# Batch 0 of a pooled-attention kernel: k by head pair over SyncE's queue, half of q over ScalarE's, v in two halves

## The chip, the cores and the metric

The kernel runs on one core of a Trainium2 chip. A core has five engines that run their own instruction streams and wait for one another by semaphores: PE (TensorE, matrix products into PSUM), DVE (VectorE) and ACT (ScalarE) for elementwise work, POOL (GpSimd), and SP (SyncE), which here only issues transfers. SP, ACT and POOL can issue DMAs; here POOL's DMAs also convert float32 to bfloat16 on the way, those of SP and ACT copy as is. The metric is the time of one execution in microseconds (us). The profiler also gives the span, from the first to the last instruction, and every start time below is counted from its beginning. All sizes in KB are those written on the chip.

## The reference

Attention over 8 batches and 8 heads of 576 tokens with head size 64, in which keys and values are first averaged over groups of 8 tokens (72 groups), and then a two-layer network on the 4608 tokens:

```python
k_p = k.reshape(B, H, Sp, pool, D).mean(axis=3)      # B=8, H=8, Sp=72, pool=8, D=64
v_p = v.reshape(B, H, Sp, pool, D).mean(axis=3)
scores = (1.0 / np.sqrt(D)) * np.matmul(q, k_p.transpose(0, 1, 3, 2))
scores = scores - np.max(scores, axis=-1, keepdims=True)
attn = np.exp(scores)
attn = attn / (np.sum(attn, axis=-1, keepdims=True) + 1e-09)
attn_out = np.matmul(attn, v_p)                      # (8, 8, 576, 64)
x = attn_out.transpose(0, 2, 1, 3).reshape(4608, 512)
h = x @ w_in                                         # 512 -> 2048
g = h * np.cos(h)
out = g @ w_out                                      # 2048 -> 512, float32
```

Inputs and output are float32.

## The kernel before

The order of the instructions on each engine is written out by hand: no scheduler moves them, and each engine takes its own in the order of the program.

**The network.** The 4608 tokens are cut into 9 tiles of 512 (`NT`), the loop variable being `t`. For a tile, `up_mm` multiplies `w_in` in 8 pieces (`fp`), each of two 128-row chunks with 4 products over k (`ki`), into one of three double banks of PSUM (`banks`); `up_g` takes the cosine on ACT and multiplies on DVE into `g_sb`. Then `down_mm` runs 64 products with `w_out` into two single banks (`obanks`), and `down_out` copies and stores. The attention of the next batch is set between these products. The weights come in four quarters each: `w_in_sb0..3` and `w_out_sb0..3`. For tile 0 the down products are ordered so that a quarter of `w_out` is first asked for at the products 0, 8, 16 and 24.

**The attention.** Batch b's result `xT` is needed by tile b (and a piece of tile b+1). Scores are worked out in four units (`us`, here by heads: two stretches of 256 tokens for heads 0 to 3, then the two for heads 4 to 7) and a rest of 64 tokens that is done later. A unit is: `scores` (products on PE, then the exponential on ACT, `ex`); `sums_first` (the denominators by PE with a matrix of ones, then logarithm and exponential of its negative on ACT, `lnc` and `inv`; there is a single `lnc` buffer); `values_then` (products with pooled v on PE, then a multiplication by `inv` on DVE into `xT`). For the later batches pooling runs on POOL; for batches 0 and 1 it runs on PE:

- `pool_k_mm` multiplies the staged k of a head pair with `groups`, a matrix of zeros and ones that DVE builds at the start (`dist`, `sign`, `groups`) from two iotas of POOL. Both halves of the partitions (a head each) land in one bank, and `put_kk` copies them into `kk`, each half into both halves of the partitions: four copies for a call of two head pairs.
- `pool_v_mm` does the same for v, 18 products of 256 columns, and one copy into `vz`.
- `q_transpose_mm` transposes 128x128 blocks of q on PE into PSUM; a copy puts them into `qT`.

**The beginning.** Before tile 0 nothing can be hidden behind the network. In the order of the program (L336 to L423): SP loads the first half of k (head pairs 0 and 1) as float32 into `k_first`, a part of `g_sb` that is not yet used, and ACT casts it in one operation (L343). POOL issues, on one queue, which works them off in order: the first half of q, then after its iotas the second halves of k and q, v whole, the first three quarters of `w_in`, k of batch 1, and so on, `w_out` last (L344 to L386). An issue on POOL waits until the eighth DMA before it has landed. PE warms up with products that nobody reads (`warm_up`, first ten, later pairs), pools the first two head pairs of k, transposes the first half of q (copies on DVE and ACT), does the scores of units 0 and 1, the second half of k and of q, and the rest as it lands (L396 to L422).

Of the kernel before, what the change touches and what calls it, by code (L numbers as in the profile page):

```python
# [9 lines left out]
FP32 = mybir.dt.float32  # L10
BF16 = mybir.dt.bfloat16
# [3 lines left out]
POOL = 8  # L15
# [4 lines left out]
def kernel(  # L20
# [9 lines left out]
    nc = tc.nc  # L30
# [94 lines left out]
    def v_part(b):  # L125
        return vz[b % 2][:, :, 0:4:3, :]

    def put_kk(b, ps, pj0, pj1, copy):
        dst = kk[b % 2].rearrange("p (j a) n -> p j a n", a=2)
        for a in range(2):  # L130
            for r in range(2):
                copy(out=dst[half[r], pj0:pj1, a, 0:Sp], in_=ps[half[a]])

# [16 lines left out]
    def pool_k_mm(b, bank, pj0, pj1):  # L150

        kb = staged["k", b]
        ps = bank[:, 0:(pj1 - pj0) * Sp].rearrange("p (j n) -> p j n", n=Sp)
        for pj in range(pj0, pj1):
            for t in range(ROW):
                for rows in half:
                    nc.tensor.matmul(ps[rows, pj - pj0, :], lhsT=kb[rows, pj, t, :], rhs=groups[rows, t, :],
                                     start=(t == 0), stop=(t == ROW - 1))
        return lambda copy: put_kk(b, ps, pj0, pj1, copy)

    def pool_v_mm(b, pair):
# [122 lines left out]
    def exp_tables():  # L284
        nc.scalar.preload_act_table_set("natural_log_exp_and_others")  # L285
# [49 lines left out]
    warm = consts.tile([128, 512], BF16, name="warm")  # L335
    nc.vector.memset(warm, 1.0)  # L336
    exp_tables()
# [3 lines left out]
    k_first = g_sb.rearrange("p f n -> p (f n)").bitcast(FP32)[:, 0:2 * ROW * D]  # L341
    nc.sync.dma_start(out=k_first.rearrange("p (j n) -> p j n", j=2), in_=even_view(k, 0, 0, 2))
    nc.scalar.copy(out=staged["k", 0][:, 0:2].rearrange("p j t d -> p (j t d)"), in_=k_first)  # L343
# [11 lines left out]
    load_even(staged["v", 0], 0, v)  # L355
# [5 lines left out]
    nc.vector.tensor_tensor(out=dist, in0=row_of.unsqueeze(2).to_broadcast([128, ROW, Sp]),  # L361
                            in1=first_of.unsqueeze(1).to_broadcast([128, ROW, Sp]), op=mybir.AluOpType.subtract)
    nc.vector.scalar_tensor_tensor(out=sign, in0=dist, scalar=1.0 - POOL, in1=dist, op0=ADD,
                                   op1=mybir.AluOpType.mult)
    nc.vector.tensor_scalar(out=groups, in0=sign, scalar1=0.0, scalar2=None, op0=mybir.AluOpType.is_le)
# [5 lines left out]
    nc.vector.memset(half_pi, math.pi / 2.0)  # L371

# [9 lines left out]
    load_even(staged["v", 1], 1, v)  # L382
    for i in range(2):
        nc.gpsimd.memset(kp2[i], 0.0)  # L384
# [3 lines left out]
    def warm_up(n, bank):  # L388

        for i in range(n):  # L390
            nc.tensor.matmul(bank, lhsT=warm[:, 0:128], rhs=warm)
# [27 lines left out]
    values_then(0, us[2], obanks[1])  # L419
    values_then(0, us[3], obanks[0])  # L420
# [4 lines left out]
    for t in range(NT):  # L425
# [41 lines left out]
        if t == 0:  # L467
            fill[1:] = [(2, S_(0, 0)), (8, lambda: pool_v_mm(1, banks[1])), (8, lambda: values(t, REST, banks[2])),
# [66 lines left out]
```

The softmax here doesn't subtract the row's maximum and nothing guards it: scores larger than these inputs give would overflow.

## Time and profile before

| what | us |
|---|---|
| median of five runs | 302.57 |
| the five runs | 302.82, 307.39, 302.57, 302.21, 302.37 |
| the profiled execution | 302.82 |
| its span | 301.0 |
| PE busy in the span | 292.9 |
| ACT busy / DVE busy | 206.0 / 171.7 |

In the beginning of the profiled execution:

| event | us |
|---|---|
| SP issues the first half of k; it lands 3.6 later | 0.75 |
| POOL issues the first half of q; it lands 6.2 later | 1.27 |
| PE's first warm-up product | 1.47 |
| PE pools the first half of k | 5.58 |
| PE transposes the first half of q | 7.55 |
| ACT's first exponential (unit 0) | 9.31 |
| ACT's last `inv` (unit 3) begins | 17.64 |
| PE begins the up projection of tile 0 | 17.19 |
| PE begins the down projection of tile 0 | 33.56 |
| PE has the second quarter of `w_out` | 38.21 |

A line of the timeline gives start, length, engine, line of the kernel, operation, output and inputs, form and count, and in brackets how long the engine had stood idle and who released it. A line of the waits gives the engine and what it worked on, what it waited for, the total, the number of times and the longest. A line of the stages gives the stretch, its length, the busy time of PE, PE's weight loads, DVE, ACT and POOL with counts, the granted share of PE's clock, the busy share of the DMA engines and the GB/s written. PE's busy time is modelled and overlaps, so it is no measure of how well PE is used.

### The profile page before, as it was taken

Reading aid. Unit: us, or ns where it says so; the run is one execution under the profiler, and the core shown is the slowest. Engines: PE = TensorE matmul, PEld = TensorE weight load, DVE = VectorE, ACT = ScalarE, POOL = GpSimd, SP = SyncE. Lnnn points to the kernel's source line nnn. Section 1 sums busy time; section 2 is a strip of 40 time slices with the busy share of each in tenths; the row PEclk is TensorE's granted clock in tenths of the full one; section 3 lists DMA queues with packets and bytes.
Section 4 is the critical chain, followed back from the end, with each engine's and each line's share of the span. In section 5 each row is a group of like instructions: output and inputs, shape, how many; then the busy total and the mean of one; then the engine's idle time right before and its main releaser. Section 6 shows DMA issues by size and latency. Waiting matters only on the chain.

```text
span 301.0 us, 4620 instructions
## 1 busy us (share of the span) xinstructions
PE 292.9 (97%) x1814; PEld 142.7 (47%) x1814; DVE 171.7 (57%) x212; ACT 206.0 (68%) x255; POOL 129.8 (43%) x92
## 2 busy tenths in 40 slices
PE   7799999999999999999999999999999999999995
PEld 2545544444544554445444544455444544444444
DVE  6558537575467446754675556654775477425712
ACT  3886897469866987688768886789668966605500
POOL 8543016993983398339913990389300000000000
PEclk9999999999999999999999999999999999999999
DMA  7999999629526951796079617791911130131023
GB/s 144 204 207 206 209 203 200 144 46 176 121 68 119 168 123 35 142 163 138 5 167 149 127 32 171 95 174 38 149 24 35 37 70 0 37 70 35 0 67 75
DMA packets 44165, 32.91 MB, mean 109 GB/s; under 512 B 22128, under 2 KB 39408, under 8 KB 44144
## 3 DMA queue, kind: packets, MB, share of 16 engines
q0 software_dynamic: 19744, 18.07, 38.4%
q1 hardware_dynamic: 24160, 14.42, 20.5%
q8 instruction: 14, 0.23, 0.3%
q10 hardware_dynamic: 240, 0.13, 0.2%
q14 instruction: 7, 0.06, 0.1%
HBM read 36.70 MB, written 9.44 MB: 153 GB/s over the span
## 4 chain that ended last, share of the span: by engine, by line
PE 86%; DMA 10%; POOL 2%; issue 0%; DVE 0%; POOLq 0%
PE obank L310 40%; PE bank L297 37%; DMA w_out_sb<-in_moe_w_out_dram 6%; PE bank L241 5%; DMA w_in_sb<-in_moe_w_in_dram 4%; PE bank L211 3%; PE bank L328 1%; POOL kv_st L84 1%; POOL kp L384 1%; POOL q_b L84 1%; POOL identity masks.py:197 0%; POOL row_of L348 0%; DVE o_sb L316 0%; POOL identity masks.py:199 0%; POOL first_of L351 0%
## 5 line engine op out<-in xcount | busy, mean ns | idle before, releaser
L310 PE MATMUL obank<-w_out_sb,g_sb 128*128 128x512 bf16 x560 | 131.4, 379 | 0.5 <-DMA w_out_sb<-in_moe_w_out_dram 0.5
L297 PE MATMUL bank<-xT,w_in_sb 128*128 128x512 bf16 x576 | 126.7, 379 | 0.0
L304 ACT ACTIVATE cos<-bank,half_pi 128x1024 f32<-128x1024 f32 x72 | 79.2, 1112 | 59.0 <-PE bank L297 59.0
L307 DVE TENSOR_TENSOR g_sb<-bank,cos 128x1024 bf16<-128x1024 f32 x72 | 87.3, 1223 | 42.5 <-ACT cos L304 42.5
L297 PEld LDWEIGHTS <-w_in_sb 128*128 128x128 bf16 x576 | 56.1, 98 | 67.7 <-issue 1.8
L310 PEld LDWEIGHTS <-g_sb 128*128 128x128 bf16 x560 | 52.9, 98 | 57.1 <-issue 2.5
L252 DVE TENSOR_TENSOR xT<-bank,inv 64x512 bf16<-64x512 f32 (+1 forms) x72 | 45.3, 630 | 41.3 <-ACT inv L248 40.6
L141 POOL TENSOR_TENSOR kv_st<-kv_st 72x2048 f32<-72x2048 bf16 x12 | 48.8, 4064 | 35.2 <-DMA kv_st<-in_k_dram 35.2
L247 ACT ACTIVATE lnc<-bank 64x512 f32<-64x512 f32 (+1 forms) x72 | 39.2, 544 | 3.2 <-PE bank L241 1.9
L316 DVE COPY o_sb<-obank 128x512 f32<-128x512 f32 x35 | 23.6, 690 | 31.0 <-PE obank L310 30.6
L218 ACT ACTIVATE ex<-bank 72x1024 bf16<-72x1024 f32 (+1 forms) x40 | 35.0, 928 | 8.9 <-PE bank L211 8.9
L142 POOL TENSOR_TENSOR kv_st<-kv_st 72x1024 f32<-72x1024 f32 x12 | 28.2, 2346 | 1.0
L248 ACT ACTIVATE inv<-lnc 128x512 f32<-128x512 f32 (+1 forms) x36 | 21.0, 583 | 1.1
L241 PE MATMUL bank<-ex,vz 72*128 72x256 bf16 (+1 forms) x176 | 20.0, 243 | 0.0
L241 PEld LDWEIGHTS <-vz 72*128 72x128 bf16 x176 | 13.6, 97 | 9.6 <-DVE xT L252 0.5
L145 POOL TENSOR_TENSOR kp<-kv_st 72x512 bf16<-72x512 f32 x12 | 15.0, 1266 | 0.5
L211 PE MATMUL bank<-qT,kk 64*72 64x256 bf16 (+1 forms) x192 | 13.4, 252 | 0.7 <-ACT qT L193 0.5
L211 PEld LDWEIGHTS <-kk 64*72 64x72 bf16 x192 | 7.5, 109 | 10.6 <-issue 7.9
L285 ACT ACT_TABLE_LOAD x9 | 11.5, 1283 | 0.9 <-PEq L519 0.8
L499 POOL COPY gate<-kk 1x1 bf16<-1x1 bf16 x5 | 0.9, 180 | 25.1 <-DMA kk<-kp 25.1
L288 ACT ACT_TABLE_LOAD x9 | 11.5, 1283 | 0.2
L84 POOL DMA_DIRECT2D q_b<-in_q_dram x10 | 7.7, 772 | 2.8 <-DMA w_in_sb<-in_moe_w_in_dram 1.4
(55 smaller groups left out, 89.2 us busy)
## 6 DMA issues: line engine op xcount, KB each, us to landing
out_dram<-o_sb SPq DMA_DIRECT2D x70, 128.0 KB, 2.4
kv_st<-in_v_dram POOLq DMA_DIRECT2D x8, 576.0 KB, 13.8
kv_st<-in_k_dram POOLq DMA_DIRECT2D x7, 576.0 KB, 7.6
q_b<-in_q_dram POOLq DMA_DIRECT2D x6, 576.0 KB, 9.8
w_in_sb<-in_moe_w_in_dram POOLq DMA_DIRECT2D x4, 512.0 KB, 13.8
w_out_sb<-in_moe_w_out_dram POOLq DMA_DIRECT2D x4, 512.0 KB, 18.4
q_b<-in_q_dram POOLq DMA_DIRECT2D x4, 288.0 KB, 12.1
g_sb<-in_k_dram SPq DMA_DIRECT2D x1, 576.0 KB, 3.6
```

Of the source, the lines that this page charges most:

```text
L141: add(out=s, in0=x[:, :, 0:4, :], in1=x[:, :, 4:8, :], op=ADD)
L142: add(out=s[:, :, 0:2, :], in0=s[:, :, 0:2, :], in1=s[:, :, 2:4, :], op=ADD)
L211: nc.tensor.matmul(pair[:Sp, bank, c:c + n].rearrange("p (g n) -> p g n", n=64), lhsT=kk[b % 2][half[r], h0 + i, 0:Sp], rhs=att["qT", b][h ...
L218: nc.scalar.activation(out=ex[:, 0:nh * n].rearrange("p (a n) -> p a n", a=2), in_=pair[:Sp, :, 0:nh * n // 2], func=ACTF.Exp, scale=scale ...
L241: nc.tensor.matmul(pair[:, hp, (i // 2) * n:(i // 2 + 1) * n], lhsT=vz[b % 2][:, pj, 2 * hp:2 * hp + 2, :].rearrange("p a d -> p (a d)"), ...
L247: nc.scalar.activation(out=lnc[half[1 - hp]], in_=pair[half[1 - hp], hp, 0:w], func=ACTF.Ln)
L252: nc.vector.tensor_mul(out=x_out(b, u, half[hp]), in0=cols(pair[half[hp], hp, :], u), in1=cols(inv[half[1 - hp]], u))
L297: nc.tensor.matmul(h[:, j, :], lhsT=w_in_sb[fc // 4][:, ki, (fc % 4) * 128:(fc % 4 + 1) * 128], rhs=xT[:, ki, t * TILE:(t + 1) * TILE], st ...
L304: nc.scalar.activation(out=cos, in_=h, func=ACTF.Sin, bias=half_pi[:, :1])
L307: nc.vector.tensor_mul(out=g_sb[:, 2 * fp:2 * fp + 2, :], in0=h, in1=cos)
L310: nc.tensor.matmul(o, lhsT=g_sb[:, fc, ms * 128:(ms + 1) * 128], rhs=w_out_sb[fc // 4][:, fc % 4, :], start=(fc == 0), stop=(fc == FFCH - 1))
L316: nc.vector.tensor_copy(out=o[:, 0:n], in_=ps)
```

## The change

- SP loads k's head pairs 0 and 1 in two DMAs, one each, and ACT issues one DMA for head pairs 0 and 1 of q, both as float32 into a part of `g_sb` (`raw`), ahead of the load of its table. ACT casts the two k pieces, DVE the two q pieces (`cast_first`). POOL no longer issues that half of q, and issues v of batch 0 in two halves.
- `pool_k_mm` and `pool_v_mm` take a bank for each half of the partitions. The k copies become two functions, one per bank, which can go to different engines; batch 1's k is pooled in one call of four head pairs.
- v of batch 0 is pooled in two calls of two head pairs, and its copies are two for each call.
- The order of the beginning is new: the first pair of k copies goes to ACT, the second to DVE; the denominators of unit 0 come before the second half of k; the copies of the second half of q all go to DVE; the first half of pooled v is set ahead of the scores of unit 2, the second half behind the values of units 0 and 1.
- The first warm-up is 8 products rather than 10, one more pair of them stands behind the scores, and their operand is 128 columns, repeated.
- DVE fills `vz[0]`, `ones` and `half_pi` before it builds `groups`; `vz[1]` is filled by POOL, just before it clears `kp2`.

```diff
-    def pool_k_mm(b, bank, pj0, pj1):
+    def pool_k_mm(b, ps, pj0, pj1):
         kb = staged["k", b]
-        ps = bank[:, 0:(pj1 - pj0) * Sp].rearrange("p (j n) -> p j n", n=Sp)
+        ps = [p[half[a], 0:(pj1 - pj0) * Sp].rearrange("p (j n) -> p j n", n=Sp) for a, p in enumerate(ps)]
         for pj in range(pj0, pj1):
             for t in range(ROW):
-                for rows in half:
-                    nc.tensor.matmul(ps[rows, pj - pj0, :], lhsT=kb[rows, pj, t, :], rhs=groups[rows, t, :],
+                for a in range(2):
+                    nc.tensor.matmul(ps[a][:, pj - pj0, :], lhsT=kb[half[a], pj, t, :], rhs=groups[half[a], t, :],
                                      start=(t == 0), stop=(t == ROW - 1))
-        return lambda copy: put_kk(b, ps, pj0, pj1, copy)
+        dst = kk[b % 2].rearrange("p (j a) n -> p j a n", a=2)
+        def put(a):
+            def go(copy):
+                for r in range(2):
+                    copy(out=dst[half[r], pj0:pj1, a, 0:Sp], in_=ps[a])
+            return go
+        return put(0), put(1)
 
-    def pool_v_mm(b, pair):
+    def pool_v_mm(b, ps, pj0=0, pj1=KCH):
         vb = staged["v", b]
+        ps = [p[:Sp, 0:(pj1 - pj0) * D] for p in ps]
         for t in range(ROW):
             for hp, rows in enumerate(half):
-                nc.tensor.matmul(pair[:Sp, hp, 0:KCH * D], lhsT=groups[rows, t, :], rhs=vb[rows, :, t, :],
+                nc.tensor.matmul(ps[hp], lhsT=groups[rows, t, :], rhs=vb[rows, pj0:pj1, t, :],
                                  start=(t == 0), stop=(t == ROW - 1))
-        nc.vector.tensor_copy(out=v_part(b).rearrange("p j a d -> p a j d"),
-                              in_=pair[:Sp, :, 0:KCH * D].rearrange("p a (j d) -> p a j d", j=KCH))
+        for hp in range(2):
+            nc.vector.tensor_copy(out=v_part(b)[:, pj0:pj1, hp, :], in_=ps[hp].rearrange("p (j d) -> p j d", d=D))
...
-    exp_tables()
     kv_even_tiles(0)
     q_tile(0)
-    k_first = g_sb.rearrange("p f n -> p (f n)").bitcast(FP32)[:, 0:2 * ROW * D]
-    nc.sync.dma_start(out=k_first.rearrange("p (j n) -> p j n", j=2), in_=even_view(k, 0, 0, 2))
-    nc.scalar.copy(out=staged["k", 0][:, 0:2].rearrange("p j t d -> p (j t d)"), in_=k_first)
-    load_even(staged["q", 0], 0, q, 0, 2)
+    raw = g_sb.rearrange("p f n -> p (f n)").bitcast(FP32)[:, 0:KCH * ROW * D].rearrange("p (i n) -> p i n", i=KCH)
+    for j in range(2):
+        nc.sync.dma_start(out=raw[:, j:j + 1], in_=even_view(k, 0, j, j + 1))
+    nc.scalar.dma_start(out=raw[:, 2:4], in_=even_view(q, 0, 0, 2))
+    exp_tables()
+    def cast_first(which, copy, j):
+        copy(out=staged[which, 0][:, j].rearrange("p t d -> p (t d)"), in_=raw[:, 2 * (which == "q") + j])
+    for j in range(2):
+        cast_first("k", nc.scalar.copy, j)
...
-    load_even(staged["v", 0], 0, v)
+    load_even(staged["v", 0], 0, v, 0, 2)
+    load_even(staged["v", 0], 0, v, 2, 4)
...
-    warm_up(10, obanks[0])
-    pool_k_mm(0, obanks[1], 0, 2)(vec)
-    warm_up(2, banks[1][:, 0, :])
-    puts = q_transpose_mm(0, banks[2][:, 0, :], 0, 5), q_transpose_mm(0, obanks[0], 5, 9)
+    warm_up(8, obanks[0])
+    puts = pool_k_mm(0, obanks, 0, 2)
+    for j in range(2):
+        cast_first("q", vec, j)
+    puts[0](act)
+    puts[1](vec)
+    warm_up(2, banks[2][:, 0, :])
+    puts = q_transpose_mm(0, banks[1][:, 0, :], 0, 5), q_transpose_mm(0, banks[0][:, 0, :], 5, 9)
     puts[0](vec)
     puts[1](act)
-    warm_up(2, banks[1][:, 0, :])
-    scores(0, us[0], banks[0])
-    scores(0, us[1], banks[1])
-    pool_k_mm(0, obanks[1], 2, 4)(vec)
-    sums_first(0, us[0], banks[0][:, 0, :])
-    puts = q_transpose_mm(0, banks[2][:, 0, :], 9, 14), q_transpose_mm(0, obanks[0], 14, 18)
-    puts[0](vec)
-    puts[1](act)
+    warm_up(2, banks[2][:, 0, :])
+    scores(0, us[0], banks[2])
+    scores(0, us[1], banks[0])
+    warm_up(2, obanks[1])
+    sums_first(0, us[0], obanks[0])
+    for put in pool_k_mm(0, [banks[1][:, i, :] for i in range(2)], 2, 4):
+        put(vec)
     sums_first(0, us[1], obanks[1])
-    scores(0, us[2], banks[0])
-    scores(0, us[3], banks[2])
-    nc.vector.memset(vz[1], float(POOL))
-    pool_v_mm(0, banks[1])
-    sums_first(0, us[2], obanks[0])
-    values_then(0, us[0], obanks[1])
-    values_then(0, us[1], banks[1][:, 0, :])
-    sums_first(0, us[3], banks[2][:, 0, :])
-    values_then(0, us[2], obanks[1])
-    values_then(0, us[3], obanks[0])
+    for put in [q_transpose_mm(0, banks[0][:, i, :], 9 + 5 * i, 14 + 4 * i) for i in range(2)]:
+        put(vec)
+    pool_v_mm(0, obanks, 0, 2)
+    scores(0, us[2], banks[2])
+    scores(0, us[3], banks[1])
+    values_then(0, us[0], obanks[0])
+    values_then(0, us[1], obanks[1])
+    pool_v_mm(0, (banks[0][:, 0, :], banks[0][:, 1, :]), 2, 4)
+    sums_first(0, us[2], banks[2][:, 0, :])
+    sums_first(0, us[3], banks[1][:, 0, :])
+    values_then(0, us[2], obanks[0])
+    values_then(0, us[3], obanks[1])
...
-                    puts = pool_k_mm(1, obanks[0], 0, 2), pool_k_mm(1, obanks[1], 2, 4)
+                    puts = pool_k_mm(1, obanks, 0, 4)
```

More of the change, by code (lines that the diff above doesn't have):

```diff
@@ L126, in v_part @@
         return vz[b % 2][:, :, 0:4:3, :]
[L128 to L132, printed above, removed]
     def pool_add(b, which):
@@ L334 @@
     EX = 5
-    warm = consts.tile([128, 512], BF16, name="warm")
+    warm = consts.tile([128, 128], BF16, name="warm")
     nc.vector.memset(warm, 1.0)
-    exp_tables()
     kv_even_tiles(0)
     q_tile(0)
-    k_first = g_sb.rearrange("p f n -> p (f n)").bitcast(FP32)[:, 0:2 * ROW * D]
-    nc.sync.dma_start(out=k_first.rearrange("p (j n) -> p j n", j=2), in_=even_view(k, 0, 0, 2))
-    nc.scalar.copy(out=staged["k", 0][:, 0:2].rearrange("p j t d -> p (j t d)"), in_=k_first)
-    load_even(staged["q", 0], 0, q, 0, 2)
+    raw = g_sb.rearrange("p f n -> p (f n)").bitcast(FP32)[:, 0:KCH * ROW * D].rearrange("p (i n) -> p i n", i=KCH)
[7 more added lines that the diff above has]
+        cast_first("k", nc.scalar.copy, j)
     row_of = consts.tile([128, ROW], FP32, name="row_of")
@@ L360 @@
     groups = consts.tile([128, ROW, Sp], BF16, name="groups")
[L361 to L365, printed above, removed]
     nc.vector.memset(vz[0], float(POOL))
@@ L371 @@
     nc.vector.memset(half_pi, math.pi / 2.0)
+    nc.vector.tensor_tensor(out=dist, in0=row_of.unsqueeze(2).to_broadcast([128, ROW, Sp]),
+                            in1=first_of.unsqueeze(1).to_broadcast([128, ROW, Sp]), op=mybir.AluOpType.subtract)
+    nc.vector.scalar_tensor_tensor(out=sign, in0=dist, scalar=1.0 - POOL, in1=dist, op0=ADD,
+                                   op1=mybir.AluOpType.mult)
+    nc.vector.tensor_scalar(out=groups, in0=sign, scalar1=0.0, scalar2=None, op0=mybir.AluOpType.is_le)
     kv_even_tiles(1)
@@ L382 @@
     load_even(staged["v", 1], 1, v)
+    nc.gpsimd.memset(vz[1], float(POOL))
     for i in range(2):
@@ L390, in warm_up @@
         for i in range(n):
-            nc.tensor.matmul(bank, lhsT=warm[:, 0:128], rhs=warm)
+            nc.tensor.matmul(bank.rearrange("p (a n) -> p a n", a=4), lhsT=warm,
+                             rhs=warm.unsqueeze(1).to_broadcast([128, 4, 128]))
     vec, act = nc.vector.tensor_copy, nc.scalar.copy
     us = BY_HEADS
-    warm_up(10, obanks[0])
-    pool_k_mm(0, obanks[1], 0, 2)(vec)
-    warm_up(2, banks[1][:, 0, :])
-    puts = q_transpose_mm(0, banks[2][:, 0, :], 0, 5), q_transpose_mm(0, obanks[0], 5, 9)
+    warm_up(8, obanks[0])
@@ L467 @@
         if t == 0:
-            fill[1:] = [(2, S_(0, 0)), (8, lambda: pool_v_mm(1, banks[1])), (8, lambda: values(t, REST, banks[2])),
+            fill[1:] = [(2, S_(0, 0)), (8, lambda: pool_v_mm(1, [banks[1][:, i, :] for i in range(2)])), (8, lambda: values(t, REST, banks[2])),
                         (11, S_(1, 0)), (13, V_(0, 1)), (18, S_(2, 2)), (21, V_(1, 0, later)), (26, S_(3, 1)),
```

## The prediction

> **What bounds the kernel now.** I read the page first: span, busy shares and slices. Then the chain that ended last, the waits of PE, the timeline of the first 22 us, and the table of stages, in that order. All times are in us from the start of the span.
>
> ```profile
> span 301.0 us, 4620 instructions
> PE 292.9 (97%) x1814; PEld 142.7 (47%) x1814; DVE 171.7 (57%) x212; ACT 206.0 (68%) x255; POOL 129.8 (43%) x92
> ```
>
> PE works nearly all the time. Nothing after the first 45 us is touched by the change except by being shifted, so the question is when PE gets through the beginning.
>
> ```profile
> 5.81 11.03 DMA w_in_sb<-in_moe_w_in_dram
> ...
> 19.73 18.43 DMA w_out_sb<-in_moe_w_out_dram
> 38.16 0.04 issue
> 38.21 0.81 PE obank L310 x3
> ```
>
> This is the chain in order of time (start, length, what). Up to 38.16 it runs through weight loads, not through the attention of batch 0; from there on it is PE alone.
>
> ```profile
> PE bank L192 <- DMA q_b<-in_q_dram: 0.7, 1, 0.7
> PE obank L310 <- DMA w_out_sb<-in_moe_w_out_dram: 0.5, 1, 0.5
> ```
>
> The waits of PE up to 45 us (total, times, longest). The second line is the one that matters: PE comes 0.46 us too early to the second quarter of w_out (ready at 37.75, starts at 38.21). So a later PE loses its first 0.46 us for free, and an earlier PE gains only what this load gains too.
>
> ```profile
> 4.37 1.15 ACT L343 CAST kv_st<-g_sb 128x1152 bf16<-128x1152 f32 x1 [2.34 <-DMA g_sb<-in_k_dram]
> 7.55 0.45 PE L192 MATMUL bank<-identity,q_b 128*128 128x128 bf16 x5 [0.66 <-DMA q_b<-in_q_dram]
> 8.26 0.58 ACT L193 COPY qT<-obank 128x512 bf16<-128x512 bf16 x1 [2.74 <-PE obank L192]
> 9.31 1.93 ACT L218 ACTIVATE ex<-bank 72x1024 bf16<-72x1024 f32 x2 [0.46 <-PE bank L211]
> 12.29 0.57 ACT L193 COPY qT<-obank 128x512 bf16<-128x512 bf16 x1
> 13.93 1.91 ACT L218 ACTIVATE ex<-bank 72x1024 bf16<-72x1024 f32 x2
> 17.64 0.63 ACT L271 ACTIVATE inv<-lnc 128x512 f32<-128x512 f32 x1
> 18.30 0.69 DVE L282 TENSOR_TENSOR xT<-obank,inv 128x512 bf16<-128x512 f32 x1 [0.50 <-ACT inv L271]
> ```
>
> From 9.31 on ACT runs without a gap to the end of `inv` at 18.27; the last product on DVE ends at 18.99, and PE's third and fourth k-chunk of the up projection start there (19.05). So the beginning is an ACT chain, set off by the first exp, which is set off by q's landing.
>
> ```profile
> 2.50:3.00 0.50, 0.50 (x3) 0.15 (x1) 0.12 (x1) 0.00 (x0) 0.43 (x3) 1.00 0.91 346
> 3.00:3.50 0.50, 0.50 (x2) 0.15 (x1) 0.50 (x1) 0.00 (x0) 0.50 (x1) 1.00 1.05 392
> 4.00:4.50 0.50, 0.50 (x3) 0.22 (x2) 0.50 (x1) 0.13 (x1) 0.50 (x2) 1.00 0.80 97
> 20.00:22.00 2.00, 2.00 (x11) 0.88 (x10) 0.74 (x1) 1.89 (x2) 0.47 (x1) 1.00 1.21 207
> ```
>
> Stages; the last two columns are DMA share and GB/s. k over SyncE's queue runs at up to 392; POOL's casting queue starts at 97 and settles at 207 written (twice that read).
>
> **Terms of the change.** (1) *q and k land together.* k's 576 KB (590 kB) were issued at 0.75 and landed 3.6 later, at 4.35; q's first half, on POOL's queue, was issued at 1.27 and landed 6.2 later, at 7.5. Now 590 kB of q go out beside k. In before the rows give 85 kB at 2.0 to 2.5 (170 GB/s), 173 and 196 kB in the next two, 454 kB by 3.5; at 392 k would end at 3.85, so landing lags by 0.5. Of 1180 kB, 726 remain at 3.5: at 392 that is 1.85, landing at 5.85 for the second half of k and for q. POOL's queue joins at about 4: with a third taken from then, 530 kB at 261 take 2.03, landing 6.53. If it kept its 97 to 122 written, some 200 read, the 530 kB would go at 190: landing 7.3. With two queues ramping up sooner I can not get below 5.4. I take L = 6.15, midway between 5.85 and 6.53, as POOL's queue is slow in just this stage.
>
> (2) *From L to the first exp.* ACT's cast of the second k pair is half of the 1.15: 0.6. PE's 18 products are half of the 36 (0.77, of which 0.2 latency): issued within 0.3. Two warm fillers take 0.43. So q's transposes start at 6.15 + 0.05 + 0.6 + 0.05 + 0.3 + 0.43 = 7.55 rounded, the same 7.55 as before. DVE casts two q pairs of 576 meanwhile; the nearest row, `groups` (648 elements from f32 in SBUF, 0.75), makes 0.67 each, half that if DVE goes twice as fast: done by 7.5 or 6.85. The put of kk, four copies on DVE (0.29, 0.95) before, is now two on DVE and two on ACT, in front of the qT copies: DVE 7.55 to 8.17, then qT 0.49; ACT 7.35 to 7.92, then qT at 8.26, as before. The first exp is at 9.31: L + 3.16. The 1.35 that q gains in landing goes into the casts and the wait for k's second pair.
>
> (3) *From the first exp (E) to xT.* The second qT copy leaves ACT (from `inv` of unit 0 to Ln of unit 1 it was 1.00 with the copy between; without it 0.66, since Ln must wait for the buffer that `inv` reads: 0.34 less). But a new wait comes in. The pooled v takes both obanks, in which the sums of units 0 and 1 lie, so its second product waits until Ln of unit 1 is done: E, +0.91 exp, +0.91 Ln, +0.63 inv, +0.66 Ln, +0.60 = E + 3.71. Behind it on PE stand 16 more v products (18 of 256 columns were 0.06 apart, of 128 half that: 0.45) and the scores of unit 2. DVE's four kk copies (1.26), the qT copies of 0.49 and 0.42 in its order, end at E + 4.38: those scores need them. Their exp starts 0.41 after the last qT: E + 4.85, where ACT is free at E + 4.28 and stood at E + 4.62 before. From there the same operations: exp 0.91, 0.89, Ln 0.63, inv 0.66, Ln 0.63, inv 0.66, mul; the last mul begins at E + 9.23, 0.24 later than before (18.30 - 9.31 = 8.99). Values of units 0 and 1, v's other half (0.5) and the sums fit on PE before each is asked for (sums of unit 2 done at E + 6.55, ACT asks at E + 6.65).
>
> (4) *The weight stream.* POOL's queue works in order at 207 GB/s. Without 295 kB of q it is 1.43 shorter; 590 kB more on the same engines at 392 cost 1.50. Bounds for the landing of w_out's second quarter: 0.1 later, or 1.43 earlier if all of q fits where POOL's queue ran at 97 to 146 anyway (4 to 7 us). Middle: 0.7 earlier. The next two quarters landed at 22.25 + 18.4 = 40.7 and 25.05 + 18.1 = 43.2, PE asked at 40.8 and 43.4; they move with it.
>
> (5) *Costed at nothing.* `vz[1]`'s memset, 0.91 on DVE, goes to POOL ahead of the issue of w_out's second quarter (19.73); that load has its turn only after v of batch 1 landed (17.12 + 18.4 = 35.5), so 15 us cover it; without them it would cost 0.9. `groups` comes after `vz[0]` and the small memsets (1.1 us), but its iotas no longer stand behind a q issue of 0.87 on POOL: done near 4.65 against 5.36, wanted at 4.9 by the first k pair. ACT's DMA issue (0.46) ahead of its table load (1.28) is over at 2.5, long before the first cast. Batch 1's k puts, 1.26 on DVE and 1.13 on ACT, become four longer copies; PE does not wait there. v's load in two pieces is one more issue on POOL (0.75), in place of q's.
>
> **The sum.** PE at the up projection: (6.15 + 3.16 - 9.31) + 0.24 = 0.24 later. It then waits less at w_out: 0.24 - 0.46 = 0.22 earlier, if the load is at least that much earlier, which (4) allows. In general the end moves by the later of (L - 6.37) and the load's shift. The profiled execution took 302.82, 1.82 around its span; that is 0.25 over the median of 302.57. So 302.60 for it, and 302.35 for the median. What the measurement can tell from no change is 0.2%, 0.6 us.
>
> [...] In before the ten warm products start 0.43 apart from 1.47, and the ninth's weight load at 4.86 is the first fast one (0.11 for 0.15), after 3.4 us of steady work; fillers at 6.28 take 0.60 for two. The change has eight, 3.4 us from about 1.15, then about 1.1 us without work while PE waits for the second k pair. [...]
>
> **Rivals.** A (*faster*): the two queues run at 392 and POOL's waits: L = 5.6, PE is 0.77 earlier at w_out, and the load is 0.7 earlier: 301.9. For: the 392 and the slow 97 of POOL's queue. Against: the engines' share is 1.05 with k alone, so they are full. Faster than 0.2% needs L under 5.77 and a load 0.6 earlier.
>
> B (*slower*): the warm state is missed, and PE's spacing of 0.43 in place of 0.215 holds through the first part. On the path to the first exp 18 products, two fillers, the transposes and the scores double: 0.3 + 0.43 + 0.28 + 0.2 = 1.2. Sum 0.24 + 1.2 - 0.46 = 1.0 later: 303.6. It decides when E is past 10.1. For: eight instead of ten, and the gap. Against: 3.4 us was just enough before, and two more fillers are put behind the scores.
>
> C (*slower*): POOL's queue keeps its rate beside the two others: L = 7.3, 0.9 later: 303.5, deciding from L = 6.97. [...]
>
> D (*no gain passed on*): weights only 0.1 earlier, 302.5 whatever E does below 9.4.
>
> **How the numbers follow.** Forecast with D, between 302.0 and 303.1: 0.52. A: 0.26. B, with waits that I have not seen: 0.15. C: 0.07. That gives 0.26, 0.52 and 0.22. The forecast's own range is 302.0 to 303.1; to leave out no more than two in ten the range takes in most of A and of B: 301.6 to 303.6.
>
> **What would show it.** Right: k's second pair and q land near 6.15, the first exp near 9.3, a wait of ACT's third exp near 0.6, PE's wait for w_out smaller than 0.46. Wrong: q's landing past 7; starts of PE 0.43 apart after 5 us (B); a PE that waits longer than 0.46 at w_out because the beginning became shorter and the load did not; or a wait on POOL's k, q or v pieces in the first 15 us, for which I have no term.

## The result: 304.01 us, in two groups

The changed kernel takes 304.01 us (median of 53 runs, 302.82 to 305.12) against 302.63 us for the kernel before (95 runs). The ratio is 1.0029, 95% interval 1.0018 to 1.0040: slower, and 0.4 us above the upper end of the predicted range. Its runs fall in two groups with nothing between 303.26 and 303.71: 20 of the 53 lie near 302.9, the other 33 near 304.2.

The ratio is that of the means, in which the kernel before keeps seven runs at 305.4 to 306.4 and only its five above 307 are left out; the bare medians stand 1.0046 apart. The ratios below can hold such runs too, so I go by medians and single times. They are a group of the kernel before's own: 12 of its 95 runs lie at 305.4 or above, and none of the changed kernel's 53. Beside the experiments, where the granted share of PE's clock is listed for each run, such runs have 0.98 to 0.99. None was traced, so what they are stays open.

The execution that was profiled (303.11 us, span 301.1) is one of the lower group. Its page begins:

```profile
span 301.1 us, 4666 instructions
PE 293.3 (97%) x1832; PEld 142.8 (47%) x1832; DVE 170.7 (57%) x214; ACT 206.1 (68%) x255; POOL 130.5 (43%) x93
```

The chain that ended last, in order of time (start, length, what):

```profile
1.21 4.96 DMA g_sb<-in_k_dram
6.16 0.02 issue
6.19 0.68 ACT kv_st L353
6.87 0.04 issue
6.91 0.48 PE obank L152 x18
7.39 0.54 PE bank L405 x2
7.93 0.50 PE bank L197 x9
...
9.52 1.93 ACT ex L223 x2
...
18.83 0.70 DVE xT L287
19.53 0.04 issue
19.57 7.10 PE bank L302 x32
```

Before, the chain ran through the weight loads up to 38.16. Now it runs through k's second pair, the cast, the first scores and the ACT chain to `xT`. The load of w_out has left it.

PE's waits up to 45 us (total, times, longest):

```profile
PE obank L152 <- ACT kv_st L353: 1.6, 2, 1.3
...
PE obank L170 <- ACT lnc L275: 0.5, 1, 0.5
PE bank L302 <- DVE xT L287: 0.4, 1, 0.4
```

The wait for w_out is gone. The longest is new: PE stands idle for 1.3 us between the two k pairs. The down product that had to wait follows the product ahead of it at once:

```profile
37.82 0.41 PE L246 MATMUL bank<-ex,vz 72*128 72x64 bf16 x8
38.06 0.81 PE L315 MATMUL obank<-w_out_sb,g_sb 128*128 128x512 bf16 x3
```

ACT's timeline (start, busy, what, idle before and its cause), and DVE's casts of q:

```profile
4.22 0.67 ACT L353 CAST kv_st<-g_sb 128x576 bf16<-128x576 f32 x1 [1.69 <-DMA g_sb<-in_k_dram]
6.19 0.67 ACT L353 CAST kv_st<-g_sb 128x576 bf16<-128x576 f32 x1 [1.29 <-DMA g_sb<-in_k_dram]
9.52 1.93 ACT L223 ACTIVATE ex<-bank 72x1024 bf16<-72x1024 f32 x2 [0.46 <-PE bank L216]
14.34 1.93 ACT L223 ACTIVATE ex<-bank 72x1024 bf16<-72x1024 f32 x2 [0.46 <-PE bank L216]
5.48 0.91 DVE L353 CAST q_b<-g_sb 128x576 bf16<-128x576 f32 x2 [1.17 <-DMA g_sb<-in_q_dram]
```

k's second pair lands at 6.16, the first exp starts at 9.52, and the third exp has its new wait of 0.46. So in this execution the beginning goes nearly as predicted. The up projection's third and fourth k-chunks start at 19.57 in place of 19.05, 0.52 later; the stall at w_out falls away, and the down product behind it starts at 38.06 in place of 38.21. PE's work ends 0.15 earlier than before. Yet the execution is 0.29 longer. Two questions follow: what the 304.2 group is, and where 0.44 us go in the other.

### The profile page after: what moved, and what is told of

The parts are those of the page before. It is cut to its first block, busy times and chain, and to the rows that moved or that the text cites. A ratio compares the mean times of both kernels' runs of the same rounds, so it can differ in the third digit from the quotient of the medians.

```text
span 301.1 us, 4666 instructions
## 1 busy us (share of the span) xinstructions
PE 293.3 (97%) x1832; PEld 142.8 (47%) x1832; DVE 170.7 (57%) x214; ACT 206.1 (68%) x255; POOL 130.5 (43%) x93
## 4 chain that ended last, share of the span: by engine, by line
PE 93%; ACT 3%; DMA 2%; issue 0%; DVE 0%; SPq 0%
PE bank L302 41%; PE obank L315 41%; PE bank L246 5%; PE bank L216 4%; DMA g_sb<-in_k_dram 2%; PE bank L333 1%; ACT ex L223 1%; ACT lnc L275 1%; ACT inv L276 1%; PE obank L152 1%; PE bank L170 0%; PE obank L197 0%; PE bank L405 0%; DVE xT L287 0%; ACT kv_st L353 0%
## 5 line engine op out<-in xcount | busy, mean ns | idle before, releaser
L103 POOL DMA_DIRECT2D kv_st<-in_v_dram x6 | 5.1, 843 | 9.4 <-PE bank L170 9.4
```

## Experiments: the upper group is PE's clock

Theory CLOCK is rival B: in some executions PE's clock isn't up, or falls back to half, while the path to the first exp runs. The rival theory QUEUE puts the group down to k's and q's transfers landing later.

**The changed kernel once more.** No edit.

> The changed kernel as it is, to see one of its slower executions. Its times on record fall into two groups, around 302.9 and around 304.1 us. Theory CLOCK: in the slower group PE misses the fast state in the beginning, since eight warm products and then a gap leave it short of work. Then a profile at about 304.1 has matmuls of 512 columns 0.43 us apart somewhere after 5.5 us, with k's second pair landing near 6.2 us as in the fast profile, and the first exp 0.5 to 1.5 us later than 9.52. Theory QUEUE: in the slower group k's second pair or q lands later, because the two queues are served in another order. Then the profile has 0.215 us spacing from 5.5 us on, and a landing at 7 us or later. A profile at about 302.9 says nothing; the times should again fall into the two groups.

All five runs lie in the upper group (303.98 to 304.31; ratio 1.0054, 1.0041 to 1.0067). PE's timeline:

```profile
6.90 0.75 PE L152 MATMUL obank<-groups,kv_st 64*64 64x72 bf16 x18 [1.24 <-ACT kv_st L353]
7.58 1.03 PE L405 MATMUL bank<-warm 128*128 128x512 bf16 x2
8.41 1.16 PE L197 MATMUL bank<-identity,q_b 128*128 128x128 bf16 x9
...
10.10 0.75 PE L216 MATMUL bank<-qT,kk 64*72 64x256 bf16 x8
```

The second pair starts at 6.90 as in the other execution (6.91), so QUEUE falls: k landed at 6.15 and q at 5.45. But 18 products take 0.75 instead of 0.48, two fillers 1.03 instead of 0.60, nine transposes 1.16 instead of 0.67. The first exp starts at 10.66, 1.14 later, and PE's work ends 1.13 later. That is CLOCK, of the size that rival B had (1.2 and 1.0).

Why it comes in some executions only is in the clock events of the traces, the times at which the granted clock changes. In these traces they stand 3.413 us apart or a multiple of that (7.68 and 11.09 in the second view below, 9.21 and 16.04 with q behind k, told below, and 296.96 us, 87 times 3.413, in the profile of the result), but where the first falls, the phase, differs: 4.86 before, 5.40 in the profile of the result, 9.77 here. Two views of windows on PE follow (window, length, PE busy, granted clock, DMA share, GB/s), cut at these events or whole steps of 3.41 ahead of them. First this execution:

```profile
2.94:6.36 3.42, 2.47 (x23) 1.00 1.04 311
6.36:9.77 3.41, 2.87 (x30) 1.00 1.17 188
```

(The clock column reads 1.00 ahead of the first recorded event, where nothing is recorded; two fillers that take 1.03 in place of 0.60 show half clock.) With 2.47 us of work in the window up to 6.36 the clock didn't rise; with 2.87 in the next it did, at 9.77. Then the changed kernel with six tiny extra loads, told below, which leave PE's work alone:

```profile
4.27:7.68 3.41, 1.71 (x42) 1.00 1.17 259
7.68:11.09 3.41, 3.41 (x22) 0.50 1.21 205
```

There the clock had risen at 4.27, the next window held 1.71 us of work because of the gap, and for the window after that the clock was half: 0.50. So there are two ways into the upper group, a rise that is missed and a fall, and in both traces the window in question holds the gap between the k pairs or part of it. The changed kernel's own runs show both: of its 33 upper ones 14 list a granted clock of 0.992 to 0.994, as the execution with the fall does (0.994), and 19 list 1.00, as the one with the missed rise does; the lower ones list 0.997 to 1.00.

**Ten warm products instead of eight.**

```diff
-    warm_up(8, obanks[0])
+    warm_up(10, obanks[0])
```

> The changed kernel with ten warm products at the start, as before the change, in place of eight. Theory CLOCK, if the count decides: the slower group goes or shrinks to less than a quarter of the executions, median 302.9, ratio to before about 1.001. CLOCK, if the gap between the two k pairs decides: still two groups, median above 303.5. QUEUE: still two groups, as many slow ones as with eight, median 304.0.

302.99 (302.86 to 304.35, 11 runs), one of the eleven in the upper group; ratio 1.0000 (0.9971 to 1.0030). The two products alone remove most of it.

**Eight, with three more in the gap.**

```diff
             for a in range(2):
...
+            if after_first is not None and pj == pj0:
+                after_first()
...
-    puts = pool_k_mm(0, obanks, 0, 2)
+    puts = pool_k_mm(0, obanks, 0, 2, lambda: warm_up(3, banks[2][:, 0, :]))
```

> The changed kernel with eight warm products at the start, and three more (0.65 us fast, 1.28 us slow) between the pooling of the first and the second head pair of k, where PE stands idle from 5.6 to 6.9 us. Theory CLOCK, gap: the slower group goes, median 302.9. CLOCK, count: the slower group goes as well, as eleven are issued before the second pair. QUEUE: two groups as before, median 304.0; nothing in the landing of k or q changes.

303.00 (302.89 to 303.12, 11 runs), none in the upper group; ratio 1.0009 (0.9987 to 1.0030). Filling the gap is enough without the two products. Two kernels below with the same filling and order, one with q's load moved and one with small extra loads, have none in 11 and 12 runs.

**The kernel before with eight.**

```diff
-    warm_up(10, obanks[0])
+    warm_up(8, obanks[0])
```

> The kernel before with eight warm products at the start in place of ten, and nothing else. Theory CLOCK, count: it gets a slower group near 303.8 to 304.2 as well, in a quarter or more of its executions. CLOCK, gap: it has no gap between two k pairs, so it stays one group at 302.6. QUEUE: one group at 302.6.

302.44 (302.13 to 306.06, 12 runs), none near 304 and two at 306.0, where the kernel before has runs too; ratio 1.0009 (0.9978 to 1.0041). Its first pooled k follows the warm products as one block of 36, and the clock is up from 6.39. So eight alone do no harm, and the gap alone little (one in eleven with ten): the change brought both.

These traces show what a window of 3.41 us held, cut at the recorded events, and what the clock did after it. It fell after 1.10 (q behind k on SyncE's queue), 1.48 (the same in the other order of batch 0), 1.81 (both k pairs in one DMA; all three told below) and 1.71 us of work, and held after 1.82 with ten products:

```profile
3.73:7.14 3.41, 1.82 (x41) 1.00 1.11 279
```

It didn't rise after 2.47 and rose after 2.87, in the execution above. Slid along the first 12 us of the profile of the changed kernel, the emptiest window holds 1.84, with three fillers in the gap 2.95, in the kernel before 2.63 (further on 2.61 and 2.27). By these points the changed kernel stands at the edge and the other two clear of it. They are few, and what the clock goes by was not shown.

## Experiments: transfers

**q behind k on SyncE's queue** (with ten warm products). The edit was meant to give k the 392 GB/s that it had alone.

```diff
-    nc.scalar.dma_start(out=raw[:, 2:4], in_=even_view(q, 0, 0, 2))
+    nc.sync.dma_start(out=raw[:, 2:4], in_=even_view(q, 0, 0, 2))
```

> The changed kernel with ten warm products, and the half of q issued on SyncE's queue behind the two k pairs instead of on ScalarE's at once. Theory SHARE: q at once is what keeps k's second pair back to 6.15 us. Then k's second pair lands at 4.2 to 4.6, q at 5.6 to 6.2, the first exp comes at 8.3 to 8.9 instead of 9.4 to 9.5, PE reaches w_out's second quarter 0.5 to 1.0 us sooner, and the median is 301.8 to 302.3 (302.9 to 303.0 with ten and nothing else). Theory BYTES: the same bytes pass the same engines in the same time, what k gains q loses, and the first exp waits for q instead: 9.2 to 9.6, median 302.8 to 303.1. Aside: the time around the span is 2.0 us in all kernels with this change and 1.8 in the one before; if the transfer on ScalarE's queue at the start makes it, it falls back to 1.8 here.

307.4 (304.86 to 307.68, 6 runs), ratio 1.0116 (1.0063 to 1.0169): both expectations fall. k landed at 3.63 and 4.28, as SHARE had it, but q at 9.82. The chain and the stages (all engines; the last three columns are granted clock, DMA share and GB/s):

```profile
1.67 8.15 DMA g_sb<-in_q_dram
```

```profile
4.00:4.50 0.50, 0.50 (x3) 0.19 (x2) 0.31 (x1) 0.50 (x2) 0.50 (x2) 1.00 0.65 184
7.00:8.00 1.00, 0.00 (x0) 0.00 (x0) 0.00 (x0) 0.00 (x0) 1.00 (x2) 1.00 1.00 191
10.00:12.00 2.00, 1.64 (x11) 1.07 (x11) 1.79 (x5) 0.46 (x1) 0.96 (x2) 0.50 1.22 207
```

At 4.0 to 4.5, as k ends and q is alone on its queue, the engines are only 0.65 busy. POOL's queue starts to move data at 5.0, and from 5.5 on q moves at 18 to 92 GB/s beside it, until 9.82. PE waits, its window holds 1.10 us of work, and the clock is at 0.50 from 9.21 to 16.04. So q over ScalarE's queue was the better place: it landed there at 5.46. Whether the other queue or the later start (1.67 for 0.75) makes it crawl wasn't separated.

**Both k pairs in one DMA** (with ten warm products).

```diff
-    for j in range(2):
-        nc.sync.dma_start(out=raw[:, j:j + 1], in_=even_view(k, 0, j, j + 1))
+    nc.sync.dma_start(out=raw[:, 0:2], in_=even_view(k, 0, 0, 2))
```

> The changed kernel with ten warm products, k's two head pairs in one DMA on SyncE's queue (the two casts stay apart), q at once on ScalarE's. If the split by head pair is worth something, both casts now wait for the later landing, near 5.5 to 6.2: the second cast ends 0.5 to 0.7 us later than in the change, the first exp comes at 9.9 to 10.2 and the median is 303.3 to 303.6. If the split is worth nothing, because k in one DMA is not kept back behind q: first exp at 9.0 to 9.5, median at or under 303.0. The number of transfers on SyncE's and ScalarE's queues before the outputs falls from three to two; if the order of the last waits on them makes the 0.2 us between the last landing and the end of the span (1.29 after, 1.07 before), that part changes here.

303.13 (303.07 to 304.58, 10 runs), four of ten at 304.1 to 304.6; ratio 1.0009 (0.9973 to 1.0044). The median lies between the two expectations. k lands whole at 5.74 and q at 6.05: earlier than the second pair's 6.16, but nothing of k comes before. The profile is one of the upper four; the window up to 7.70 holds 1.81 us of PE's work there, and in the next the clock is at 0.50:

```profile
4.29:7.70 3.41, 1.81 (x41) 1.00 1.15 274
7.70:11.12 3.42, 3.42 (x22) 0.50 1.21 206
```

**q's load after the table load in ScalarE's program** (with the gap filled; once in the changed order, once in that of the next section). This was to give k a head start.

```diff
-    nc.scalar.dma_start(out=raw[:, 2:4], in_=even_view(q, 0, 0, 2))
     exp_tables()
+    nc.scalar.dma_start(out=raw[:, 2:4], in_=even_view(q, 0, 0, 2))
```

> The change with eight warm products and three fillers in the gap, and ScalarE's load of q issued after its table load, at about 2.0 us instead of 0.75. Theory SHARE: q beside k is what holds k's second pair back, so it lands at 4.3 to 5.0 instead of 6.1, q at 5.8 to 6.4, the first exp is at 8.5 to 9.0 instead of 9.4, and the median 302.2 to 302.6 (303.0 with the fillers alone). Theory STARVE: a transfer of these queues that still has much to move when POOL's queue begins to move data (at 5.0 us) crawls from there on, as q did behind k on SyncE's queue, where it landed at 9.2 to 9.8; then q lands after 7.5, the first exp is past 10.3 and the median 303.8 or more.

> The order and the fillers of the first kernel of this set, with q issued after the table load. SHARE: first exp at 8.5 to 9.0, PE ready for w_out's second quarter at 36.4 to 37.0, where it waits for the load at 37.0 to 37.4; median 301.8 to 302.2, the best of all. STARVE: first exp past 10.3, median 303.3 or more.

303.04 (ratio 1.0009, 0.9994 to 1.0024) and 302.70 (1.0015, 1.0001 to 1.0029). They tell nothing about the head start: ScalarE issued q at 0.79 and 0.78, beside the table load (0.75 to 2.03), not after it. The first has none of 11 runs in the upper group, the second three of 12 at 304.1 to 304.3, which the next section takes up.

## Experiments: the order of batch 0

**Pooled v behind the scores** (with ten warm products). The second half of k is pooled right after the first scores, in place of the last two fillers; scores of units 2 and 3 go ahead of the pooled v, whose two halves stand together ahead of the sums of unit 2 and the values.

```diff
-    warm_up(2, obanks[1])
-    sums_first(0, us[0], obanks[0])
     for put in pool_k_mm(0, [banks[1][:, i, :] for i in range(2)], 2, 4):
         put(vec)
+    sums_first(0, us[0], obanks[0])
     sums_first(0, us[1], obanks[1])
...
-    pool_v_mm(0, obanks, 0, 2)
     scores(0, us[2], banks[2])
     scores(0, us[3], banks[1])
+    pool_v_mm(0, obanks, 0, 2)
+    pool_v_mm(0, (banks[0][:, 0, :], banks[0][:, 1, :]), 2, 4)
...
```

> The changed kernel with ten warm products, q at once beside k as it is, and another order behind the first scores: the second half of k is pooled right after the scores of unit 1 in place of two fillers, the scores of units 2 and 3 come before any pooled v, and both v halves before the values. This takes away the wait of ACT's third exp (about 0.55 us in the profile of the change). Theory CHAIN: the beginning is ACT's chain from the first exp on, so xT is ready 0.5 to 0.65 us sooner, and as the weights now land 1 us sooner than before the change, all of it arrives at the end: median 302.3 to 302.5. Theory STREAM: the weights bind, PE meets the wait for w_out again and the median stays at 302.8 to 303.0.

302.51 (302.42 to 304.10, 12 runs), three of them at 303.8 to 304.1; ratio 0.9977 (0.9941 to 1.0013). ACT's third exp:

```profile
13.81 1.93 ACT L223 ACTIVATE ex<-bank 72x1024 bf16<-72x1024 f32 x2
```

It starts 4.40 after the first (4.82 in the changed kernel) and without a wait: CHAIN holds. The lower group is 0.48 below that of the ten products alone. So the wait that the prediction's step 3 named is real and costs PE about its whole length (0.46), since the load of w_out no longer swallows it.

**With both edits**, this order and q behind k on SyncE's queue:

> Both edits together: ten warm products, q behind k on SyncE's queue, and the order with the scores of units 2 and 3 ahead of pooled v. If SHARE and CHAIN hold, PE would be ready for w_out's second quarter 1.5 us sooner than in the change as it is (38.06), at about 36.5, but that quarter lands at 37.1 to 37.3. So STREAM decides here: PE waits 0.5 to 0.8 us for it and the median is 301.7 to 302.0, no better than with q behind k alone. If no load binds: 301.2 to 301.5.

306.4 (304.35 to 308.28), ratio 1.0106 (1.0042 to 1.0170): q landed at 9.21, and the order can't help that.

**Where the new order's upper runs come from.** Ten products and three in the gap, in this order:

> The change with the order of the earlier run (second half of k pooled right after the first scores, scores of units 2 and 3 ahead of pooled v), ten warm products, and three fillers between the two first k pairs. Theory CLOCK, gap: without the gap no execution falls into the group 1.2 us higher, of which the same order without the fillers had three of twelve (303.8 to 304.1): all of them between 302.3 and 302.8, median 302.5. If the gap is not the cause, two to four of twelve are above 303.5 again.

302.57, still two of eleven at 304.4 (ratio 1.0003, 0.9978 to 1.0029). The order took two fillers away, and PE waits 0.50 and 0.66 after the first scores:

```profile
11.28 0.41 PE L273 MATMUL obank<-ex,ones 72*64 72x256 bf16 x4 [0.50 <-ACT ex L225]
12.96 0.93 PE L218 MATMUL bank<-qT,kk 64*72 64x256 bf16 x8 [0.66 <-DVE qT L200]
```

The emptiest 3.41 us of the first 14 lie there, with 2.00 of work. Two warm products in each of these waits:

```diff
+    warm_up(2, banks[2][:, 0, :])
     sums_first(0, us[1], obanks[1])
     for put in [q_transpose_mm(0, banks[0][:, i, :], 9 + 5 * i, 14 + 4 * i) for i in range(2)]:
         put(vec)
+    warm_up(2, banks[2][:, 0, :])
     scores(0, us[2], banks[2])
```

> The other order of batch 0 with the three products in the gap of the k pairs, and two more warm products in each of the two later waits of PE (ahead of the sums of unit 1, 0.50 idle, and ahead of the scores of unit 2, 0.66 idle). Theory WAITS (the slow first part comes back where PE has some half of a us without work anywhere in the first 14 us): no execution near 304.4, the median 302.5 to 302.7. Theory GAP ONLY: the same share near 304.4 as without the two pairs of products, 2 of 11. Both expect nothing on the path to the first exp, which starts at 9.4.

302.50 (302.42 to 302.82, 12 runs), none above; nor in twelve runs of the same kernel with small extra loads, below. Without the two pairs it was five of 23, with q's load after the table load counted in. That agrees with WAITS; the emptiest 3.41 us now hold 2.94. None of this order's upper runs was traced. That they are the clock again is inferred from the granted clock that the runs list: 0.992 to 0.994 in these five, 0.997 to 1.00 in the lower ones. Of the three with ten products alone one has 0.992, the other two 0.998.

## Experiments: what takes 0.44 us outside PE's work

**The kernel before with three transfers instead of one.** Two unread loads of 32 KB behind k on SyncE's queue, so that three transfers on the SyncE and ScalarE queues stand ahead of the outputs, as in the changed kernel.

```diff
+    spare = consts.tile([128, 2, D], FP32, name="spare")
+    for i in range(2):
+        nc.sync.dma_start(out=spare[:, i, :], in_=moe_w_in[0:128, i * D:(i + 1) * D])
```

> The kernel before, with two small loads (32 KB each, of weights, that nobody reads) on SyncE's queue behind k, so that three transfers stand on SyncE's and ScalarE's queues before the outputs, as in the change, and not one. Theory ENDING: the eight semaphores that these transfers use in turn are awaited one after the other at the end, and with three the last landing meets them at another place: 1.29 from the last landing to the end of the span and 2.0 around the span, instead of 1.07 and 1.80, so the median is 302.9 to 303.1 although the beginning does not change. Rival: the beginning of the changed kernel itself costs these 0.4 us; then it stays at 302.5 to 302.7.

303.00 (302.82 to 303.19, 11 runs), ratio 1.0017 (1.0008 to 1.0026): slower, though nothing else is changed. The last copy of the output on DVE, first in the kernel before, then with the two loads:

```profile
297.56 0.29 DVE L316 COPY o_sb<-bank 128x128 f32<-128x128 f32 x1 [0.60 <-PE bank L328]
```

```profile
span 301.3 us, 4591 instructions
297.63 0.29 DVE L316 COPY o_sb<-bank 128x128 f32<-128x128 f32 x1 [0.60 <-PE bank L328]
```

From its start to the end of the span it is 3.46 before (span 301.02), 3.67 in the changed kernel (297.42 to 301.09) and 3.69 here (to 301.32). So some 0.22 of the 0.44 come with the two added transfers, with no other edit.

**Nine transfers.** The transfers of these two queues use eight semaphores in turn to report their landing: 89 landings in the trace of the kernel before and 91 in that of the result, 11 or 12 on each of the eight. If the outputs' place in this round of eight decides, nine ahead of them is as good as one. Six unread loads of 1 KB behind k's, in three kernels:

```diff
+    spare = consts.tile([4, 6, D], FP32, name="spare")
+    for i in range(6):
+        nc.sync.dma_start(out=spare[:, i, :], in_=moe_w_in[0:4, i * D:(i + 1) * D])
```

The changed kernel with the gap filled:

> The changed kernel with three more warm products between the first two k pairs, and six unread loads of 1 KB on SyncE's queue behind k, so that nine transfers stand ahead of the outputs on the SyncE and ScalarE queues instead of three (before has one). Theory ROUND (what costs at the end is the outputs' place in a round of eight transfers, and nine is the same place as one): from the last output's landing to the end of the span 1.07 instead of 1.29, and the time 302.7 to 302.85 if only that goes, 302.5 to 302.65 if the 0.2 around the span goes with it. Theory COUNT (each transfer ahead of the outputs costs): the end takes 1.5 or more, and the time is 303.2 to 303.8.

302.76 (302.62 to 303.00, 12 runs), ratio 0.9994 (0.9964 to 1.0023). Without the loads it was 303.00, but in another set of runs, in which the kernel before stood at 302.60; beside this one it stands at 302.43. So the times leave only 0.07. The traces decide: from the last copy to the end it is 3.47 here and 3.68 without the loads.

The changed kernel itself:

> The changed kernel, nothing else altered, with the six unread loads of 1 KB. ROUND: both groups of its times move down together, from 302.9 and 304.1 to 302.6 and 303.85 (302.45 and 303.7 if the 0.2 around the span goes too), with the slow first part in some half of the executions as before. COUNT: both move up by 0.2 to 0.8.

Five of twelve at 302.62 to 302.73, seven at 303.44 to 304.03: the lower group is 0.25 lower than in the result, of which the kernel before, at 302.63 then and 302.43 now, accounts for 0.2. The upper group is there as before. The end takes 3.45.

The other order with all waits filled:

> The same kernel with the six unread loads of 1 KB. ROUND: 302.25 to 302.4, or 302.05 to 302.2 if the 0.2 around the span goes too, and an end of 1.07. COUNT: 302.9 to 303.4.

302.28 (302.19 to 302.63, 12 runs) against 302.50 without the loads, here in the same set of runs; ratio to the kernel before 0.9973 (0.9941 to 1.0006). The last copy:

```profile
296.77 0.29 DVE L323 COPY o_sb<-bank 128x128 f32<-128x128 f32 x1 [0.60 <-PE bank L335]
```

The span is 300.22 long, so this end takes 3.45 again, for 3.68 without the loads. By the ends ROUND holds and COUNT falls in all three, by the times in the pair of one set. The kernel with both k pairs in one DMA, with two transfers ahead of the outputs, fits too: its end takes 3.72, more than with nine. Other places in the round weren't tried. The time around the span, which is an execution's time less its span, didn't go back: 2.00, 1.99 and 2.05 us in these three.

That second 0.2 us stays open. The time around the span is 1.77 to 1.80 in the four traced kernels that load k's half in one DMA (before, before with eight, before with three transfers, both pairs in one DMA) and 1.99 to 2.05 in all that load it by pairs. The split goes along with it. The transfer on ScalarE's queue doesn't make it: with q behind k on SyncE's queue it is 2.02, and with both pairs in one DMA, where q stays on ScalarE's queue, 1.77. What of the split makes it wasn't tried.

No version beat the kernel before by what the prediction said a measurement can tell (0.2%). The best, at 302.28, is 0.15 us below the 302.43 of the kernel before beside it, and its interval includes no change.

## Why the prediction was wrong, step by step

**What bounded the beginning** was read rightly: the ACT chain set off by the first exp, and w_out's load as the second limit.

**Step 1**, the landing: L = 6.15 was forecast, 6.16 came. That the number fits is partly luck. The working let POOL's queue take a third from about 4. That share was an estimate, and no run shows it: POOL's queue moved nothing until 4.90, then 76 of 260 GB/s from 5.0 to 5.5 and 145 of 187 in the next half us; q, on its own queue, went ahead (309 GB/s beside 37 from 3.0 to 3.5) and landed at 5.46, and k's second pair landed after it (at 4.28 when q stood behind it). The middle of 5.85 and 6.53 is 6.19 besides. Rivals A (5.6) and C (7.3) fall.

**Step 2**, L to the first exp: 3.16 forecast, 3.36 came. The cast of a k pair took 0.67, not 0.6, and PE's 18 products held up the next ones by 0.41, not 0.3; the terms listed also make 7.58 where 7.55 was written. The casts of q on DVE took 0.46 each, between the 0.67 and its half that were given.

**Step 3**, the new wait: E + 4.85 was forecast for the third exp, E + 4.82 came; the last product at E + 9.23 came at E + 9.31. The sum of steps 2 and 3 is 0.52 later at the up projection, against 0.24.

**Step 4**, the weights: 0.7 earlier was forecast, 1.08 came (landing 37.08 instead of 38.16). **The sum's wait at w_out** was worth 0.67, not the 0.46 used: PE was 0.52 later at the up projection and 0.15 earlier behind the wait. So −0.15 came of the sum of PE's steps, in place of −0.22. All that step 5 costed at nothing was covered; none of it stands in the chain or among PE's waits.

**The step that failed is the sum without a term for PE's clock**, and with it the chance of 0.15 for rival B. The row had shown that the ninth product's weight load was the first fast one, in one execution, and I took this for a length of work that eight products would just cover. It was one draw of a phase: the clock event of that trace stands at 4.86 as well. Against B stood "3.4 us was just enough before, and two more fillers are put behind the scores"; the fillers lie after the path that counts, and eight products with 1.3 us of idle time behind them fail in three executions of five. E at 10.66 is past the 10.1 that rival B gave as its point of decision, and its 1.0 to 1.2 us came as 1.13 and 1.14 in the traced execution. The forecast of 302.35 had also no term for the end: 0.22 through the two added transfers, and 0.2 around the span. They turn the lower group's gain of 0.15 into the 0.29 by which its profile is longer.

The half clock came back without an idle window, too: in the changed kernel with six tiny extra loads the window ahead of it held 1.71 us of work and no idle time longer than 1.34.

## What to carry to other kernels

Here a load split at the start left PE 1.3 us without work, and 33 of 53 runs fell into the upper group. After such a change count PE's busy time in every 3.4 us stretch of the first 15 us, at every phase, not in the one execution that the profile shows. Look at the single times before trusting one profile: where they fall in two groups with a gap between them, as here, take a profile of each. And where the gain is tenths of a us, compare the end of the span and the time around it too: here two transfers added at the start, with no other edit, took the end from 3.46 to 3.69.

## What the runs showed of the hardware that was not expected

- The clock of PE fell after 1.10, 1.48, 1.71 and 1.81 us of work in a window of 3.41 us, and held after 1.82; it didn't rise after 2.47 and rose after 2.87.
- Two transfers on two queues were not served alike: q on ScalarE's queue landed at 5.46, k's second pair, issued 0.46 later on SyncE's, at 6.16; in the three half us from 3.0 to 4.5 the trace's packets show 37, 23 and 92 GB/s for k's queue beside 309, 382 and 286 for q's. And q, last on SyncE's queue and beside POOL's, landed at 9.82 (8.15 us for 590 kB) where it took 4.7 on ScalarE's queue.
- The load of q that stands behind the table load in ScalarE's program was issued at 0.79, 0.04 after the start of that table load, which took 1.28.
- One transfer ahead of the outputs or nine: 3.45 to 3.47 us from the last copy to the end. Two: 3.72, in one trace. Three: 3.67 to 3.69.
